# Two key-weight loads on ScalarE's queue, a later gate column, other dummies and a wider last weight load in a two-branch linear attention

## The chip, the cores and the metric

The kernel runs on one core of a Trainium2 chip. The metric is the device time of one launch in microseconds (us); the profile's own clock starts at the first instruction ("span"). Names of the engines in the profile: PE is TensorE's matmul, PEld its weight load, DVE VectorE, ACT ScalarE, POOL GpSimd, SP SyncE. SPq and ACTq are instructions with which SyncE and ScalarE issue transfers (DMAs).

## The reference, cut to what matters

Two branches A and B of linear attention over the same input x (2048 rows, 640 features, 32 heads of 20), mixed by a gate:

```python
def branch(x, wqkv, wo):                       # A_wqkv, A_wo or B_wqkv, B_wo
    q, k, v = split(x @ wqkv)                  # 32 heads of 20
    phi = lambda t: where(t > 0, t + 1, exp(t)) + 1e-6
    pq, pk = phi(q), phi(k)
    kv = einsum("bhsd,bhse->bhde", pk, v)
    z = einsum("bhsd->bhd", pk)
    num = einsum("bhqd,bhde->bhqe", pq, kv)
    den = einsum("bhqd,bhd->bhq", pq, z)[..., None] + 1e-6
    return (num / den) @ wo
g = sigmoid((A_x * gate_w).sum(-1, keepdims=True))
out = g * branch(A_x, A_wqkv, A_wo) + (1 - g) * branch(A_x, B_wqkv, B_wo)
```

All inputs and the output are bf16.

## The kernel before, in words

x is cut into 16 tiles of 128 rows and 5 chunks of 128 features. The kernel needs x both as it is (`XN`) and transposed (`XT`). Tiles 0 and 1 are loaded plainly and transposed on TensorE by a multiplication with a unit matrix (`x_tp`, L478), their copies out of PSUM go to VectorE for tile 0 and to ScalarE for tile 1 (L495). Tiles 2 to 15 are transposed by the DMA (`xt_dma`).

Keys come first. A key step (`k_step`, L534 and L535) multiplies one chunk of one x tile with the 640 key columns of the same chunk of `wqkv` (tile `WKW`), as 512 and 128 columns. For tiles 0 and 1 the steps of branch A run chunk by chunk, both tiles for each chunk, so that each weight chunk is used as soon as it has landed; then branch B does the same. `gate_col` (L515) transposes the gate weights on TensorE, and a copy on VectorE (L518) puts them as a 641st key column beside each chunk's weights; branch B's steps compute the gate's argument with it. From tile 2 on, `k_both` (L612) does both branches at once. `k_post` turns keys into phi(k).

Then, per branch, phi(k) transposed times x gives a matrix of 640 x 641 (`g_unit`, L720 and L721), query tiles are computed between (`q_unit`, L874), and `kv_unit` (L782) multiplies the value weights (`WV`, as the stationary operand, loaded into TensorE in groups of 128 columns) with that matrix: five groups of 120 result columns, and a sixth that is narrower, loaded with 104 columns and 40 result columns. `wp_burst` (L817) folds the result with `wo`, its rows pass through DRAM and come back as `WPA` and `WPB`, and the output matmuls (L1034) follow.

The order is made by a small planner (`Sched`): TensorE runs its instructions in the order of the program text; the other engines choose among what is ready by priority and assumed costs; transfers of the loading phase are issued in program order on their queue. All transfers are issued at L353. SyncE's queue carries nearly all: x tile 0, the five key-weight chunks of A, the five of B, then the transposing loads of x tiles 2 to 15, the rest of x, query, value and output weights. ScalarE's queue carries x tile 1 and the gate weights; behind these on ScalarE stand the activation table's load (L384) and the copies of x tile 1. At the very start TensorE multiplies ones (`warm`, L465): these are dummies, four of 512 columns, one of 256, and one of 128 between the transposes of tile 0 and tile 1. GpSimd clears pads (L399 for `WV`).

```python
    for c in range(NC):
        if c == 0:
            ld_x("SP", c)
        ld_wk("SP", "A", c)
    for c in range(NC):
        ld_wk("SP", "B", c)
```

Of the kernel before, what the change touches and what calls it, by code (L numbers as in the profile page):

```python
# [6 lines left out]
ACT = mybir.ActivationFunctionType  # L7
# [4 lines left out]
D = 640  # L12
# [3 lines left out]
NC = 5  # L16
EPS = 1e-6
XS = ("A", "B")
GR = 120
# [57 lines left out]
class Sched:  # L77
# [7 lines left out]
    def op(self, eng, fn, cost, ins=(), outs=(), after=(), prio=None, name="", dma=None):  # L85
        if eng == "ACT" and dma is None:
            after = list(after) + self.consts
        o = Op(eng, fn, cost, list(ins), list(outs), after, len(self.ops) if prio is None else prio, name, dma)
        self.ops.append(o)
        return o  # L90
# [174 lines left out]
def body(nc, A_x, A_wqkv, A_wo, B_x, B_wqkv, B_wo, gate_w, out, log=None):  # L265
# [7 lines left out]
    bf, f32 = dt.bfloat16, dt.float32  # L273
    sb = nc.alloc_sbuf_tensor
# [3 lines left out]
    WKC = WKW[:, 0 : NC * 2 * KB_W].rearrange("p (c x f) -> p c x f", c=NC, x=2)  # L278
    WK = {X: WKC[:, :, i, :] for i, X in enumerate(XS)}
    WQ = {X: sb("WQ" + X, [128, NC, D], bf) for X in XS}  # L280
    WV = {X: sb("WV" + X, [128, NC, D + 8], bf) for X in XS}
    WO = {X: sb("WO" + X, [128, NU, D], bf) for X in XS}
    PKS = sb("PKS", [128, 2, NT * D], bf)
    PK = {X: PKS[:, i, :] for i, X in enumerate(XS)}
# [23 lines left out]
    PQ["B", 3] = GSf[:, 0:2560].rearrange("p (g s) -> p g s", g=NC)  # L308
    FXT = {"A": WV["A"][:, :, :].rearrange("p c f -> p (c f)")[:, 0:2048].rearrange("p (b s) -> p b s", b=NB), "B": XNf[:, 0:2048].rearrange("p (b s) -> p b s", b=NB)}
    NOA = 15  # L310
# [29 lines left out]
    op = sch.op  # L340

    def psw(b, w):
        return PS[:, b.slot : b.slot + b.n, :].rearrange("p a b -> p (a b)")[:, 0:w]
# [3 lines left out]
    def dma(q, name, dst, src, nbytes, ins=(), outs=(), after=(), issue=450.0, transpose=False, prio=None):  # L347
        timing = (330.0, 1500.0) if not transpose else (140.0, 1500.0) if loading else (1000.0, 1150.0)

        def fn(e):  # L350
            d = dst() if callable(dst) else dst
            with nc.allow_non_contiguous_dma(reason="layout"):
                return e.dma_start(d, src() if callable(src) else src, transpose=transpose)  # L353

        o = op(q, fn, 0.0, ins, outs, after, prio=prio, name=name, dma=(issue, nbytes) + timing)
        if loading:
            o.behind = chain.get(q)
            chain[q] = o
        return o
# [7 lines left out]
    def dve1(n):  # L367
        return 155 + 1.04 * n

    def dve4(n):  # L370
# [22 lines left out]
        outs=[bid],  # L393
        name="idn",
    )
    zgw = op("POOL", lambda e: e.memset(GWZ[:, :], 0.0), 200.0, name="zgw")
    bpad = {X: Buf("pad") for X in XS}
    for X in XS:
        op("POOL", lambda e, X=X: e.memset(WV[X][:, :, 0:4], 0.0), 300.0, outs=[bpad[X]], prio=10**6, name="wvpad")  # L399
    bxo = Buf("xo")  # L400
    op("POOL", lambda e: e.memset(XN[:, :, D : D + 1], 1.0), 200.0, outs=[bxo], name="xones")

    def ld_x(q, t):
        dma(q, "x%d" % t, XN[:, t, 0:D], x[128 * t : 128 * t + 128, :], 163840, outs=[bxn[t]])

    def ld_wk(q, X, c, after=()):
        dma(q, "wk%s%d" % (X, c), WK[X][:, c, 0:D], wqkv[X][128 * c : 128 * c + 128, D : 2 * D], 163840, outs=[bwk[X, c]], after=after)
# [13 lines left out]
    def w3(X, k):  # L421
        return wqkv[X][:, k * D : k * D + D].rearrange("(c p) f -> p c f", p=128)
# [4 lines left out]
    for c in range(NC):  # L427
        if c == 0:
            ld_x("SP", c)
        ld_wk("SP", "A", c)  # L430
    for c in range(NC):
        ld_wk("SP", "B", c)
    for t0, t1 in ((2, 3), (3, 4), (4, 5), (5, 6), (6, 8), (8, 12), (12, 16)):
# [4 lines left out]
    for X in XS:  # L438
        dma("SP", "wv" + X, WV[X][:, :, 4 : D + 4], w3(X, 2), 819200, outs=[bwv[X]])
    for X in XS:  # L440
        for r in range(2):
# [7 lines left out]
                outs=[bwo[X, r]],  # L449
# [11 lines left out]
    def warm(n, w=4):  # L461
        for i in range(n):
            op(
                "PE",
                lambda e: e.matmul(psw(bw, 128 * w), ONE[:, 0:1].to_broadcast([128, 128]), ONE[:, 0:1].to_broadcast([128, 128 * w]), start=True, stop=True),  # L465
                107.0 * w,
                ins=[bone],
                outs=[bw],
                name="warm",
            )  # L470

    def x_tp(t):
        for lo, hi in ((0, 1), (1, 3), (3, 5)):
            bt = Buf("tp", "ps")
            for c in range(lo, hi):
                op(
                    "PE",
                    lambda e, c=c, lo=lo, bt=bt: e.matmul(  # L478
                        PS[:, bt.slot, 128 * (c - lo) : 128 * (c - lo) + 128],
                        XN[:, t, 128 * c : 128 * c + 128],  # L480
                        IDN[:, :],
                        start=True,
                        stop=True,
                    ),
                    100.0,
                    ins=[bxn[t], bid],
                    outs=[bt],
                    name="tp%d" % t,
                )
            half = Buf("xth")  # L490

            def copy(e, lo=lo, hi=hi, bt=bt):
                o = XT[:, lo:hi, 128 * t : 128 * t + 128]
                i = PS[:, bt.slot, 0 : 128 * (hi - lo)].rearrange("p (c s) -> p c s", c=hi - lo)
                return e.activation(o, i, ACT.Copy) if t else e.tensor_copy(o, i)  # L495

            op(
                "ACT" if t else "DVE",
                copy,
                act_cost(128 * (hi - lo)) if t else dve1(128 * (hi - lo)),  # L500
                ins=[bt],
                outs=[half],
                name="tpc%d" % t,
            )
            bxt[t].parts = getattr(bxt[t], "parts", []) + [half] * (hi - lo)
# [3 lines left out]
    def gate_col():  # L509
        bt = Buf("gwp", "ps")  # L510

        def tv():
            return PS[:, bt.slot, 0:NC]

        op("PE", lambda e: e.matmul(tv(), GWZ[:, :], IDN[:, 0:NC], start=True, stop=True), 60.0, ins=[bgw, bid], outs=[bt], name="gwt")  # L515
        op(
            "DVE",
            lambda e: e.tensor_copy(WKC[:, :, :, D : D + 1], tv().unsqueeze(2).unsqueeze(3).to_broadcast([128, NC, 2, 1])),  # L518
            170.0,
            ins=[bt],  # L520
            outs=[bgc],
            name="gwc",
        )
# [143 lines left out]
        clamp(768, 1280, [eb], tb)  # L667
        add(PKt["B"][:, t, 0:512], lambda: bank(2), lambda: ekw(768, 1280), 2, [tb], [pk["B"]])

    warm(4)  # L670
    warm(1, 2)
    pss = [Buf("k", "ps", 2) for _ in range(2)]
    x_tp(0)
    warm(1, 1)
    x_tp(1)
    for c in range(2):
        for t in range(2):
            k_step("A", t, c, pss[t])
    gate_col()
    for c in range(2, NC):  # L680
        for t in range(2):
            k_step("A", t, c, pss[t])
    for t in range(2):
# [7 lines left out]
    for t in range(2, NT):  # L691
# [12 lines left out]
        outs=[bgg2],  # L704
        prio=LOW + 52,
        name="gm",
# [47 lines left out]
    def kv_unit(X):  # L754
        gv = GS[X][:, :, :].rearrange("p c (g m) -> p c g m", g=NC)

        def out(src, u0, n, w, mask, r0, r1):
            b = Buf("kvl")
            bkvl[X].append(b)
            op(  # L760
                "DVE",
                lambda e: e.tensor_tensor(
                    out=KVL[X][r0:r1, u0 : u0 + n, 0 : w * NC].rearrange("p u (m g) -> p u g m", g=NC),
                    in0=src().rearrange("p (u g m) -> p u g m", u=n, g=NC),
                    in1=mask.unsqueeze(1).unsqueeze(1).to_broadcast([r1 - r0, n, NC, w]),
                    op=ALU.mult,
                ),
                dve1(w * NC * n),
                ins=[ps, bcst],
                outs=[b],  # L770
                prio=-1,
                name="kvm",
            )

        for us in ((0, 1, 2, 3), (4, 5)):
            ps = Buf("kv", "ps")

            def fn(e, us=us, ps=ps):
                for i, u in enumerate(us):
                    for c in range(NC):  # L780
                        lo, n, w = (GR * u, 128, 24) if u < 5 else (540, 104, 8)
                        r = e.matmul(  # L782
                            PS[0:n, ps.slot, GR * i : GR * i + NC * w],
                            WV[X][:, c, lo : lo + n],
                            gv[:, c, :, 24 * u : 24 * u + w],
                            start=(c == 0),
                            stop=(c == NC - 1),
                        )
                return r

            o = op("PE", fn, 5 * len(us) * 55.0, ins=[bwv[X], bpad[X]] + [bgs[X, g] for g in range(NC)], outs=[ps], name="kv" + X)
            if X == "A":
                kv_op[X].append(o)
            n = min(us[-1], 4) - us[0] + 1
            out(lambda ps=ps, n=n: PS[:, ps.slot, 0 : GR * n], us[0], n, 24, BDM, 0, 128)
            if 5 in us:
                out(lambda ps=ps: PS[64:104, ps.slot, GR : GR + 40], 5, 1, 8, BDE, 64, 104)
# [427 lines left out]
```

## Time and profile before

| | us |
|---|---|
| device time, median of 3 runs | 187.89 (187.56 to 188.15) |
| span of the profiled execution | 186.1 |
| median less span | 1.8 |
| PE busy in it | 183.1 |
| DVE / ACT / POOL busy | 137.2 / 96.5 / 0.8 |

Of the profiled execution the profile gives the span; the time around it is taken as the difference to the median of the runs. In a line of the timeline the first number is the start in us from the span's start, the second the duration, then the engine, the line of the kernel, the operation, what it writes and reads (`out<-in`), its shape and how many instructions are merged; in brackets stands how long the engine was idle before it, and what ended that. In the chain, each line is a piece of the path that ended last, in order of time. Groups give durations in ns as minimum, median and maximum. Matmul durations overlap, since matmuls are pipelined; the pace is read from the starts.

### The profile page before, as it was taken

How to read it: one execution, taken by the hardware profiler on the slowest of the kernel's cores; microseconds unless marked ns; L12 is line 12 of the kernel's file. 1: busy time of each engine (PE TensorE's matmuls, PEld its weight loads, DVE VectorE, ACT ScalarE, POOL GpSimd, SP SyncE). 2: the span in 40 equal slices, each digit the busy share in tenths (PEclk: the TensorE clock that was granted, in tenths of full speed). 3: DMA queues.
4: the chain of work that ended last, by engine and by line, in shares of the span. 5: the costliest groups of instructions: out<-in, count | busy, mean ns of one | idle time of the engine just before them, and what ended most of it. 6: DMA issues, size and time to landing. Idle time of an engine off the chain costs nothing.

```text
span 186.1 us, 3137 instructions
## 1 busy us (share of the span) xinstructions
PE 183.1 (98%) x1227; PEld 105.2 (57%) x1227; DVE 137.2 (74%) x278; ACT 96.5 (52%) x181; POOL 0.8 (0%) x10
## 2 busy tenths in 40 slices
PE   8999999999999999999999999999999999999995
PEld 4555554555555556555557555555567555555553
DVE  2389888888733555487889899999899998159563
ACT  5266656665554546544675666888623784400001
POOL 1000000000000000000000000000000000000000
DMA  7979999997006011010501402125515247523334
GB/s 203 291 147 166 252 386 365 341 180 153 4 0 39 0 35 35 4 35 16 104 0 39 86 18 46 32 50 162 178 39 118 58 92 170 178 73 113 137 109 140
DMA packets 36501, 21.37 MB, mean 115 GB/s; under 512 B 25694, under 2 KB 36230, under 8 KB 36486
## 3 DMA queue, kind: packets, MB, share of 16 engines
q1 hardware_dynamic: 36188, 20.97, 44.8%
q8 instruction: 9, 0.15, 0.3%
q10 hardware_dynamic: 298, 0.20, 0.3%
q14 instruction: 6, 0.05, 0.1%
HBM read 10.87 MB, written 4.26 MB: 81 GB/s over the span
## 4 chain that ended last, share of the span: by engine, by line
PE 96%; DMA 2%; SPq 1%; DVE 0%; issue 0%; DVEq 0%
PE ps L1034 23%; PE ps L874 23%; PE ps L612 20%; PE ps L720 19%; PE ps L721 5%; DMA WKW<-in_A_wqkv_dram 2%; PE ps L534 2%; PE ps L782 2%; PE ps L817 1%; SPq L353 1%; PE ps L535 0%; DVE TSB L1078 0%; DVEq L237 0%
## 5 line engine op out<-in xcount | busy, mean ns | idle before, releaser
L720 PE MATMUL ps<-XN,PKS 128*128 128x512 bf16 x160 | 46.9, 379 | 0.0
L891 ACT ACTIVATE EK<-ps 128x512 bf16<-128x512 f32 x40 | 23.9, 598 | 30.2 <-PE ps L874 30.2
L612 PE MATMUL ps<-WKW,XT 128*128 128x512 bf16 (+1 forms) x210 | 38.1, 344 | 0.0
L721 PE MATMUL ps<-XN,PKS 128*128 128x129 bf16 x160 | 35.2, 220 | 0.0
L612 PEld LDWEIGHTS ps<-WKW,XT 128*128 128x128 bf16 x210 | 20.3, 97 | 17.5
L720 PEld LDWEIGHTS ps<-XN,PKS 128*128 128x128 bf16 x160 | 18.8, 117 | 15.8
L649 DVE SCALAR_TENSOR_TENSOR PKS<-ps,EK 128x512 bf16<-128x512 f32 (+1 forms) x42 | 24.0, 599 | 1.0
L874 PE MATMUL ps<-XT,WQA 128*128 128x512 bf16 x100 | 24.5, 379 | 0.0
L874 PE MATMUL ps<-XT,WQB 128*128 128x512 bf16 x100 | 23.8, 380 | 0.0
L901 DVE TENSOR_SCALAR EK<-EK 128x512 bf16<-128x512 bf16 x40 | 11.6, 289 | 14.1 <-ACT EK L891 14.0
L721 PEld LDWEIGHTS ps<-XN,PKS 128*128 128x128 bf16 x160 | 18.8, 117 | 3.1
L1034 PE MATMUL ps<-WPA,EX 128*128 128x512 bf16 x120 | 17.0, 299 | 0.0
L1034 PE MATMUL ps<-WPB,PKS 128*128 128x512 bf16 x120 | 16.5, 299 | 0.0
L874 PEld LDWEIGHTS ps<-XT,WQB 128*128 128x128 bf16 x100 | 10.9, 118 | 8.6 <-issue 0.4
L874 PEld LDWEIGHTS ps<-XT,WQA 128*128 128x128 bf16 x100 | 10.6, 117 | 8.1
L1034 PEld LDWEIGHTS ps<-WPB,PKS 128*128 128x128 bf16 x120 | 9.2, 98 | 7.2
L1034 PEld LDWEIGHTS ps<-WPA,EX 128*128 128x128 bf16 x120 | 9.1, 98 | 7.1 <-issue 0.4
L1080 ACT ACTIVATE TSB<-ps 128x512 bf16<-128x512 f32 x1 | 0.6, 597 | 21.9 <-PE ps L1034 21.9
L898 ACT ACTIVATE PKS<-ps 128x512 bf16<-128x512 f32 x20 | 11.9, 595 | 0.0
L639 DVE TENSOR_SCALAR EK<-EK 128x768 bf16<-128x768 bf16 (+1 forms) x28 | 9.0, 321 | 3.9 <-ACT EK L629 3.9
L666 ACT ACTIVATE EK<-ps 128x512 bf16<-128x512 f32 x14 | 8.4, 597 | 6.6 <-PE ps L612 6.6
L625 ACT ACTIVATE EK<-ps 128x512 bf16<-128x512 f32 x14 | 8.4, 597 | 6.4 <-PE ps L612 6.4
(80 smaller groups left out, 199.5 us busy)
## 6 DMA issues: line engine op xcount, KB each, us to landing
out_dram<-TSB SPq DMA_DIRECT2D x15, 160.0 KB, 1.8
XN<-in_A_x_dram SPq DMA_DIRECT2D x1, 2240.0 KB, 9.1
WKW<-in_A_wqkv_dram SPq DMA_DIRECT2D x5, 160.0 KB, 4.1
WKW<-in_B_wqkv_dram SPq DMA_DIRECT2D x5, 160.0 KB, 3.9
WQA<-in_A_wqkv_dram SPq DMA_DIRECT2D x1, 800.0 KB, 10.7
WQB<-in_B_wqkv_dram SPq DMA_DIRECT2D x1, 800.0 KB, 12.0
WVA<-in_A_wqkv_dram SPq DMA_DIRECT2D x1, 800.0 KB, 11.9
WVB<-in_B_wqkv_dram SPq DMA_DIRECT2D x1, 800.0 KB, 13.8
```

What stands on the lines that cost most here:

```text
L612: x = e.matmul(two() if i == 1 else bank(i), XT[:, c, 128 * t : 128 * t + 128], r, start=(c == 0), stop=(c == NC - 1))
L625: op("ACT", lambda e: e.activation(ekw(0, 512), bank(0), ACT.Exp), act_cost(512), ins=[ps[0]], outs=[ek, ea], name="ke")
L639: lambda e: e.tensor_scalar(ekw(lo, hi), ekw(lo, hi), 1.0, EPS, op0=ALU.min, op1=ALU.add),
L649: lambda e: e.scalar_tensor_tensor(dst, src(), 0.0, e1(), op0=ALU.max, op1=ALU.add),
L666: op("ACT", lambda e: e.activation(ekw(768, 1280), bank(2), ACT.Exp), act_cost(512), ins=[ps[2]], outs=[ek, eb], name="ke")
L720: e.matmul(a[:, 0:512], l, XN[:, t, 0:512], start=(t == 0), stop=(t == NT - 1))
L721: return e.matmul(a[:, 512 : D + 1], l, XN[:, t, 512 : D + 1], start=(t == 0), stop=(t == NT - 1))
L874: r = e.matmul(PS[:, ps.slot, :], WQ[X][:, c, g::5], XT[:, c, 512 * b : 512 * b + 512], start=(c == 0), stop=(c == NC - 1),)
L891: lambda e: e.activation(EQ[:, eq.slot, :], PS[:, ps.slot, :], ACT.Exp),
L898: op("ACT", lambda e: e.activation(PQ[X, b][:, g, :], PS[:, ps.slot, :], ACT.Relu), act_cost(512), ins=[ps], outs=[rq], name="qr")
L901: lambda e: e.tensor_scalar(EQ[:, eq.slot, :], EQ[:, eq.slot, :], 1.0, EPS, op0=ALU.min, op1=ALU.add),
L1034: r = e.matmul(a[:, l0 - lo : h0 - lo], PQ[X, b][:, g, 128 * (t % 4) : 128 * (t % 4) + 128], WP[X][:, g, l0:h0], start=(X == first and g = ...
```

## The change

Four edits. (1) Branch A's key-weight chunks 1 and 3 are issued on ScalarE's queue, behind the gate weights; chunks 0, 2 and 4 stay on SyncE's. (2) `gate_col` comes after four chunks of branch A instead of two. (3) The first dummies are five instead of four of 512 columns, followed by the same one of 256; the one of 128 columns between the two tiles' transposes is gone. (4) The last key-value group loads 128 columns instead of 104; `WV` grows by 20 columns, and GpSimd clears a second pad of 24 columns in each branch's `WV`. Its extra result rows are not read.

```diff
-    WV = {X: sb("WV" + X, [128, NC, D + 8], bf) for X in XS}
+    WV = {X: sb("WV" + X, [128, NC, D + 28], bf) for X in XS}
...
-        op("POOL", lambda e, X=X: e.memset(WV[X][:, :, 0:4], 0.0), 300.0, outs=[bpad[X]], prio=10**6, name="wvpad")
+        for lo, hi in ((0, 4), (D + 4, D + 28)):
+            op("POOL", lambda e, X=X, lo=lo, hi=hi: e.memset(WV[X][:, :, lo:hi], 0.0), 300.0, outs=[bpad[X]], prio=10**6, name="wvpad")
...
-        ld_wk("SP", "A", c)
+        ld_wk(("SP", "ACT")[c % 2], "A", c)
...
-    warm(4)
+    warm(5)
     warm(1, 2)
     pss = [Buf("k", "ps", 2) for _ in range(2)]
     x_tp(0)
-    warm(1, 1)
     x_tp(1)
-    for c in range(2):
+    for c in range(4):
         for t in range(2):
             k_step("A", t, c, pss[t])
     gate_col()
-    for c in range(2, NC):
+    for c in range(4, NC):
...
-                        lo, n, w = (GR * u, 128, 24) if u < 5 else (540, 104, 8)
+                        lo, n, w = (GR * u, 128, 24) if u < 5 else (540, 128, 8)
```

## The prediction

> **What bounds the kernel now.** I read the busy table first, then the chain of waits, then the timeline of the first 10 us, then the landings of the key-weight loads.
>
> ```profile
> span 186.1 us, 3137 instructions
> ...
> PE 183.1 (98%) x1227; PEld 105.2 (57%) x1227; DVE 137.2 (74%) x278; ACT 96.5 (52%) x181; POOL 0.8 (0%) x10
> ```
>
> TensorE (PE) is idle for only 3.0 us of 186.1. So a gain must either fill one of these holes or shorten TensorE's own work. The chain says where the holes are:
>
> ```profile
> 0.00 0.40 SPq L353
> ...
> 0.45 0.41 SPq L353
> ...
> 0.91 0.43 SPq L353
> ...
> 1.38 4.14 DMA WKW<-in_A_wqkv_dram
> ...
> 5.57 0.39 PE ps L534
> ```
>
> Up to 5.57 the end of the kernel hangs on SyncE (SP) issuing loads and on the third one, branch A's key-weight chunk 2 (issued at 1.38, landed 4.14 later at 5.52). From 5.57 the chain is TensorE alone until a copy of 0.29 at 184.08. The start is the first place to look. TensorE's part of it in the timeline:
>
> ```profile
> 1.99 0.42 PE L465 MATMUL ps<-ONE 128*128 128x256 bf16 x1
> 2.60 0.69 PE L478 MATMUL ps<-IDN,XN 128*128 128x128 bf16 x5 [0.19 <-DMA XN<-in_A_x_dram]
> 3.08 0.32 PE L465 MATMUL ps<-ONE 128*128 128x128 bf16 x1
> ```
>
> and, in the same timeline, the steps of branch A:
>
> ```profile
> 4.69 0.39 PE L534 MATMUL ps<-WKW,XT 128*128 128x512 bf16 x1 [0.24 <-DMA WKW<-in_A_wqkv_dram]
> ...
> 5.25 0.17 PE L515 MATMUL ps<-IDN,GWZ 128*128 128x5 bf16 x1
> ...
> 5.57 0.39 PE L534 MATMUL ps<-WKW,XT 128*128 128x512 bf16 x1 [0.16 <-DMA WKW<-in_A_wqkv_dram]
> ```
>
> Two stalls: chunk 1 (step starts at 4.69) and chunk 2 (5.57). The gate column's transpose at 5.25 lies inside the second. From 5.57 a key step (512 + 128 columns) comes every 0.27 (five from 5.57 to 6.94), and branch B's first step starts at 7.21.
>
> Landings, each issue time plus its time to landing: chunk 0 0.45+2.9=3.35; chunk 1 0.91+3.7=4.6; chunk 2 5.52; chunk 3 1.86+4.1=5.95; chunk 4 2.33+4.05=6.4; B0 2.81+4.0=6.8; B4 4.70+3.9=8.6; x tile 2 by transpose 5.18+4.1=9.3 (used at 9.94). From chunk 2 on they come about 0.43 apart. The table by stages says whether the DMA engines or the issues set that pace (columns: stretch, length, busy of five engines, clock, DMA share, GB/s):
>
> ```profile
> 2.50:3.00 0.50, 0.40 (x5) 0.43 (x6) 0.10 (x1) 0.23 (x2) 0.00 (x0) 1.00 1.02 368
> 3.00:3.50 0.50, 0.50 (x7) 0.50 (x6) 0.50 (x3) 0.00 (x0) 0.00 (x0) 1.00 1.19 207
> 3.50:4.00 0.50, 0.50 (x7) 0.30 (x5) 0.37 (x2) 0.46 (x2) 0.00 (x0) 1.00 0.66 128
> 4.00:4.50 0.50, 0.45 (x4) 0.12 (x2) 0.00 (x0) 0.41 (x2) 0.00 (x0) 1.00 0.78 264
> ```
>
> From 2.0 to 3.0 about 374 GB/s flow (380, then 368), with ScalarE's queue still delivering x tile 1. Then SP's queue alone feeds the engines, and 3.0 to 4.5 has a hole: mean (207+128+264)/3 = 200. Missing: 174 GB/s x 1.5 us = 0.26 MB, or **0.70 us** at 374. Every later landing carries that delay.
>
> **The change, part by part.** All times are on this execution's span, 186.08; the median of the runs, 187.89, lies 1.81 above it, and I add that at the end.
>
> *Chunks 1 and 3 on ScalarE's queue.* SP issues every 0.47 (0.45, 0.91, 1.38). Two issues fewer bring everything behind them on SP forward: chunk 2 to 0.91, chunk 4 to 1.38, B0 to 1.86, the first transposing load from 5.18 to about 4.24. ScalarE (ACT) issues its loads after the gate weights (0.70+0.52=1.22): chunk 1 at 1.25, chunk 3 at 1.72. Chunk 1 is thus issued 0.34 later than now, chunk 3 0.14 earlier. Behind them on ScalarE stand the table load (1.25, takes 1.28), a 0.20 activation, and the copies of x tile 1 (from 3.54). The table moves to 2.19, the activation ends at 3.68, the first copy starts at 3.70 instead of 3.54; so tile 1's first step goes from 4.02 to about 4.17. Today the 0.24 and 0.16 waits for weights behind it would hide that; if the weights come early, it is what is late next. Branch A then ends no earlier than 4.17 + 9 steps x 0.273 + 0.056 for the gate transpose (the pace of 128 columns, 5.80 to 5.85) = 6.68 against 7.21: **at most 0.53 gained**. B0 must have landed by then (6.8 now, so 0.17 earlier), x tile 2 by 9.4 (9.3 now, and issued 0.9 earlier).
>
> What the landings do is the unknown. *No gain:* the engines are full (share 1.0) and bytes are the same, so 0. *Whole hole filled:* 0.70 earlier, capped to 0.53. *Loss:* chunk 1, first needed, lands behind others (rival 2). The nearest row with loads on both queues is 2.0 to 3.0, without a hole; so I take most of it, 0.52 of 0.70: chunk 2 lands at 5.0, its step starts at 5.05, and six steps and the gate transpose end at 6.75. That is **0.46 gained**; half the hole (0.35) would give 5.23+1.64+0.06=6.93, gain 0.28.
>
> The Trainium skill speaks against this edit: "DMA: Bandwidth & Descriptors", section "Issuing engines are not separate DMA queues", says loads issued by different engines end on the same 16 DMA engines, so that a second issuer saves only issuing time. By that alone this part would be worth about 0 less the gate's 0.06. The hole with engines at shares of 0.66 and 0.78 is why I don't follow it fully.
>
> *Gate column later.* Its 0.056 lay in a stall; now it is on busy TensorE between chunks 3 and 4 (already in the sums). Its copy on VectorE starts 0.21 after it and takes 0.20 (5.25, 5.46, done 5.66); branch B's first step, which needs it, starts 0.056+0.546=0.60 after it. Cover 0.19; without it, 0 to 0.1 lost.
>
> *Dummies.* Five of 512 columns and one of 256 instead of four and one, and the 128-column one at 3.08 goes. They start 0.43 apart, so the 256 one moves from 1.99 to 2.41 and streams 0.21, to 2.62; the transposes begin at about 2.63 instead of 2.60, and the second five at 3.17 instead of 3.19. Zero, unless the pace (128 columns each 0.107 before 3.6, 0.056 later) doubles at another time: each 0.1 us of slow pace costs 0.05 either way. I take 0.
>
> *128 columns in the last key-value group.* 30 matmuls take 1.54 (99.98 to 101.52). 25 of them have 120 columns, at 0.0525 by the pace of 128 columns: 1.31. The five of 40 columns with 104-column loads take 0.23, 0.046 each.
>
> ```profile
> L782 PEld LDWEIGHTS ps<-GSA,WVA x30: 97/98/128, 99.8 to 101.4; 128*128 128x128 bf16 x25, 128*104 128x104 bf16 x5
> L782 PE MATMUL ps<-GSA,WVA x30: 183/216/217, 100.0 to 101.5; 128*128 128x120 bf16 x25, 128*104 128x40 bf16 x5
> ```
>
> The narrower load is the longer one, 128 ns against 98. This combination isn't in the trace: at worst 0.0525 each as beside 120 columns (0.03 lost per unit), at best the stream of 40 columns, 0.0175 (0.14 gained). Loads 30 ns shorter bring 0.046 near that end; I take 0.10, twice (branch A at 100, branch B at 141.6), **0.20**; both ends: -0.06 to 0.28. The Trainium skill, "TensorE: Matmul & The Clock Gate", section "Weight-path perf modes — Fast Weight Load (FWL) and DoubleRow", says the fast load is on at 128 weights, which fits the two rows; its floor of 25 ns between small matmuls (section "Wait — 56ns, not 53.3ns?") would make it 0.21 for both units as an estimate.
>
> *Pads.* Two more memsets on GpSimd of 0.11 to 0.14 each, 0.2 busy in all before 1.5; first needed at 99.8. Zero.
>
> *What is late next downstream.* The tightest load: WPB is issued at 156.66 and lands 4.4 later at 161.06; its first weight load is at 161.6. If the VectorE and SP work before it didn't move along, only some 0.5 of the gain would pass; most of it is released by TensorE and moves. I charge 0.
>
> **Sum:** 0.46+0.20=0.66; 186.08-0.66+1.81 = **187.2**.
>
> **Rivals.** *1, bandwidth decides:* the hole comes from what the packets wait for, whichever queue they are on. Chunk 2 still lands at 5.52; the start loses 0.06, the key-value units give 0.20: 187.75. For it: the DMA share is about 1.0 from 2.0 to 3.0 and after 4.5, and the hole's 1.19 in its first half us means packets that take long. Against: the hole begins when only one queue is left. *2, chunk 1 falls behind (slower):* its later issue and a shared turn on the engines let chunks 2, 4 and perhaps B0 pass. In fifth place (5.52) branch A ends at 5.57+8x0.273+0.06=7.81, 0.60 late, net +0.40: 188.3. In sixth (5.95): 8.24, net +0.83: **188.7**. It decides, beyond 0.3% (0.56 us, about what a measurement of this kernel can tell from no change), once chunk 1 lands after 5.7. For it: it is issued 0.34 later, behind x tile 1 and the gate weights. Against: x tile 1, issued on ScalarE at 0.12, landed only 0.4 after x tile 0. *3, the 128-column load brings nothing:* forecast less 0.20: 187.4.
>
> **Chances.** Forecast 0.55 (its own range 187.0 to 187.5, part of it within 0.3%), rival 1 0.25, rival 2 0.13, rival 3 0.07. Faster by over 0.3% (under 187.33): 0.48, 0.45 of it the forecast's and 0.03 of rival 3. Slower by over 0.3%: 0.10, rival 2 from the sixth place on. The rest, 0.42, within. The range starts at the full caps (0.53+0.28, 187.08, less 0.1 for the pace) and ends at rival 2's milder form: 187.0 to 188.3.
>
> **What would show it.** Right: chunk 2's step before 5.1, branch B's first step at 6.7 to 6.8, no DMA wait behind 4.5, no stretch of 0.5 us under 250 GB/s between 3 and 4.5; last key-value matmuls under 0.03 apart; first ScalarE copy at 3.7. Wrong: chunk 2 at 5.5 again (rival 1), a wait for chunk 1 longer than 0.5 (rival 2), a wait for the gate copy before branch B, a wait for WPB at 161.

## The result and the profile after

The changed kernel is slower: 190.58 us (189.19 to 191.14, six runs) against 187.61 (187.21 to 188.15, six runs of the kernel before on the same chip), a ratio of 1.0148 [1.0126, 1.0170]; the medians differ by 2.97 us. Ratios, here and below, compare mean times and leave out launches more than 1.5% above the same kernel's fastest, which are two of e0's and one each of e5's, e7's and e9's. The forecast was 187.2, and the time lies above the range. The profiled execution took 190.29 with a span of 188.9, 2.8 longer than the span before. First the page's total and busy times and the start of the chain of waits of the changed kernel:

```profile
span 188.9 us, 3117 instructions
...
PE 183.7 (97%) x1204; PEld 106.0 (56%) x1227; DVE 137.2 (73%) x278; ACT 96.4 (51%) x181; POOL 1.1 (1%) x12
```

```profile
1.25 5.02 DMA WKW<-in_A_wqkv_dram
6.40 0.59 PE ps L535
```

The chain no longer begins with SyncE's issues. It hangs on chunk 1, which ScalarE issues at 1.25 and which lands 5.02 later at 6.27; before, it landed at 4.65. TensorE's timeline in the changed kernel, over the first steps (`L535` is the 512-column matmul of a key step; the first line is chunk 0's second step, the others lie behind the wait for chunk 1):

```profile
4.25 0.63 PE L535 MATMUL ps<-WKW,XT 128*128 128x512 bf16 x1
...
6.40 0.59 PE L535 MATMUL ps<-WKW,XT 128*128 128x512 bf16 x1 [1.41 <-DMA WKW<-in_A_wqkv_dram]
...
6.89 0.63 PE L535 MATMUL ps<-WKW,XT 128*128 128x512 bf16 x1
...
7.43 0.63 PE L535 MATMUL ps<-WKW,XT 128*128 128x512 bf16 x1
...
9.63 0.41 PE L535 MATMUL ps<-WKW,XT 128*128 128x512 bf16 x1
...
9.93 0.38 PE L535 MATMUL ps<-WKW,XT 128*128 128x512 bf16 x1
...
10.20 0.38 PE L535 MATMUL ps<-WKW,XT 128*128 128x512 bf16 x1
```

The last line is branch B's first step. In the kernel before it is this one:

```profile
7.21 0.38 PE L534 MATMUL ps<-WKW,XT 128*128 128x512 bf16 x1
```

Two things are to be seen. TensorE idles 1.41 us for chunk 1. And the steps behind it begin 0.53 apart (6.89 to 7.43) until about 9.6, and 0.27 apart (9.93 to 10.20) only from there; before, they were 0.27 apart from the third step on. Branch B's first step starts at 10.20 instead of 7.21, 2.99 later. The key-value units give 0.1 each back, and 2.99 - 0.2 is the 2.8 of the spans. With chunk 1 at 6.40 and the pace of 0.27, branch B would have begun at 6.40 + 8 x 0.27 + 0.06 = 8.6: so 1.4 of the 2.99 is **late weights** and 1.6 is **slow pace**.

The stages of the changed kernel in which the kernel before had its hole (columns as before; the last two are the DMA share and GB/s), then the last of these stages in the kernel before:

```profile
3.00:3.50 0.50, 0.50 (x7) 0.50 (x6) 0.50 (x2) 0.49 (x2) 0.00 (x0) 1.00 1.06 202
3.50:4.00 0.50, 0.50 (x5) 0.37 (x4) 0.47 (x2) 0.50 (x3) 0.00 (x0) 1.00 0.93 115
4.00:4.50 0.50, 0.50 (x3) 0.26 (x2) 0.00 (x0) 0.41 (x2) 0.00 (x0) 1.00 0.50 138
4.50:5.00 0.50, 0.49 (x2) 0.00 (x0) 0.00 (x0) 0.00 (x0) 0.00 (x0) 1.00 0.74 220
```

```profile
4.50:5.00 0.50, 0.31 (x3) 0.19 (x4) 0.00 (x0) 0.00 (x0) 0.00 (x0) 1.00 0.93 338
```

The hole was to be filled by the second queue. In this launch it is deeper and longer: from 3.0 to 5.0 the DMA engines move 338 KB ((202+115+138+220)/2) instead of 468 KB ((207+128+264+338)/2). All later landings slip: chunk 2 5.90 (5.53 before), chunk 4 6.76 (6.38), chunk 3 7.19 (5.95), branch B's five from 7.39 (6.80) on. Of the 16 landings that the trace has for each chunk, chunk 2's have their median at 3.69 and the last at 5.90: a few parts are late, and a chunk counts from its last part.

The last edit did what it was to do. The groups of the value-weight matmuls, branch A:

```profile
L782 PEld LDWEIGHTS ps<-GSA,WVA x30: 95/98/98, 102.8 to 104.4; 128*128 128x128 bf16 x30
L782 PE MATMUL ps<-GSA,WVA x30: 179/216/216, 103.0 to 104.4; 128*128 128x120 bf16 x25, 128*128 128x40 bf16 x5
```

No load of 128 ns is left, the five matmuls of 40 columns start 0.025 to 0.028 apart (0.029 to 0.049 before), and the unit's piece of the chain takes 1.43 instead of 1.52.

### The profile page after: what moved, and what is told of

Same layout as the page of the kernel before. It is cut to its first block, busy times and chain, and to the rows that moved or that the text cites. A ratio compares the mean times of both kernels' runs of the same rounds, so it can differ in the third digit from the quotient of the medians.

```text
span 188.9 us, 3117 instructions
## 1 busy us (share of the span) xinstructions
PE 183.7 (97%) x1204; PEld 106.0 (56%) x1227; DVE 137.2 (73%) x278; ACT 96.4 (51%) x181; POOL 1.1 (1%) x12
## 4 chain that ended last, share of the span: by engine, by line
PE 95%; DMA 3%; issue 1%; POOL 0%; DVE 0%; POOLq 0%; DVEq 0%
PE ps L1034 23%; PE ps L874 23%; PE ps L613 20%; PE ps L720 18%; PE ps L721 5%; PE ps L535 3%; DMA WKW<-in_A_wqkv_dram 3%; PE ps L782 2%; PE ps L817 1%; PE ps L536 1%; POOL IDN L388 0%; DVE TSB L1078 0%; POOL WVA L400 0%; POOL XN L402 0%; POOL const-float32-0.0 L1210 0%
## 5 line engine op out<-in xcount | busy, mean ns | idle before, releaser
L720 PE MATMUL ps<-XN,PKS 128*128 128x512 bf16 x154 | 45.8, 379 | 0.1
L1034 PE MATMUL ps<-WPA,EX 128*128 128x128 bf16 (+1 forms) x117 | 16.6, 297 | 0.3 <-issue 0.2
L1034 PE MATMUL ps<-WPB,PKS 128*128 128x512 bf16 (+1 forms) x117 | 16.3, 297 | 0.2
```

What stands on the lines that cost most here:

```text
L720: e.matmul(a[:, 0:512], l, XN[:, t, 0:512], start=(t == 0), stop=(t == NT - 1))
L1034: r = e.matmul(a[:, l0 - lo : h0 - lo], PQ[X, b][:, g, 128 * (t % 4) : 128 * (t % 4) + 128], WP[X][:, g, l0:h0], start=(X == first and g = ...
```

## The experiments

Theory 1: the whole loss comes from the queue edit, by two terms, the late chunks and a slow pace that the idle time at 4.7 to 6.4 keeps. Its rivals: the new dummies or the later gate column hold the pace down; the pace is the launch's luck. Later runs ask why the chunks land late: because two queues share the engines, because ScalarE issues late, or because of the gate weights. Ratios are to the kernel before, measured beside each. Single launches of 684 us (e1), 243 us (e14) and 193.5 us (the kernel before, beside e8, e9 and e11) are left aside.

**e1: the queue edit alone**, on the kernel before.

```diff
-        ld_wk("SP", "A", c)
+        ld_wk(("SP", "ACT")[c % 2], "A", c)
```

> The kernel before with the first edit alone: chunks 1 and 3 of branch A on ScalarE's queue. Theory 1 (the queue does it all, in two terms): the chunks of both queues share the engines and land together late (chunk 1 at about 6.3 instead of 4.6), worth +1.4 us, and TensorE's idle hole before it keeps its pace slow, worth up to another +1.6. Then 190.3 to 190.9 us, near the changed kernel plus the 0.2 that its key-value units gain. Rival (the dummies or the later gate column do part of it): below 189.5 us.

Measured 188.68, ratio 1.0068 [1.0038, 1.0098]. The queue edit alone costs, but 1 us, not 3. In its profile chunk 1's step waits 0.85 and starts at 6.01, the pace is already 0.27 there, and branch B starts at 8.22. One of seven launches took 190.48. So the late chunks cost something in each of the seven (the lowest is 188.17, the median of the kernel before 187.65), the slow pace shows in one: that half of the expectation fell.

**e2: the change without the queue edit.**

```diff
-        ld_wk(("SP", "ACT")[c % 2], "A", c)
+        ld_wk("SP", "A", c)
```

> The changed kernel with all key-weight chunks back on SyncE's queue; the later gate column, the longer dummies and the 128-column load stay. Theory 1: 187.3 to 187.6 us, 0.0 to 0.3 below the kernel before (0.2 gained in the key-value units, 0.06 lost on the gate column). Rival (dummies or gate column cost something): above 188.2 us.

Measured 187.45, ratio 0.9990 [0.9969, 1.0011]. Gate column, dummies and wide load together cost nothing that can be told from zero.

**e3: the change with dummies in the idle time**, three of 512 columns between the steps of chunk 0 and those of chunk 1.

```diff
             k_step("A", t, c, pss[t])
+        if c == 0:
+            warm(3)
```

> The changed kernel with three more dummies of 512 columns on TensorE between the steps of chunk 0 and chunk 1, where it stood idle from 4.8 to 6.4. The loads are untouched. Theory 1 (idling keeps the pace slow): the landings stay late, but the pace doubles by 7.1 in every run: 188.9 to 189.4 us, 1.2 to 1.6 below the changed kernel, and the runs lie within 0.8 us. Rival (the pace has nothing to do with the idle stretch, or the loss is all in the landings): 190.3 to 190.8 us, no change.

Measured 188.72 (188.10 to 189.12), ratio 1.0057 [1.0038, 1.0076]. No launch is near 190.6. What is left, 1.1, is the late chunks less the key-value gain. Since e1, measured beside it, has only one of seven launches near 190.6, these six alone don't settle the pace; e7 and e14 do.

**e4: the wide load alone**, with its second pad, on the kernel before.

```diff
-    WV = {X: sb("WV" + X, [128, NC, D + 8], bf) for X in XS}
+    WV = {X: sb("WV" + X, [128, NC, D + 28], bf) for X in XS}
...
-                        lo, n, w = (GR * u, 128, 24) if u < 5 else (540, 104, 8)
+                        lo, n, w = (GR * u, 128, 24) if u < 5 else (540, 128, 8)
```

> The kernel before with the fourth edit alone, the 128-column load of the last key-value group and its pads. Theory: each key-value unit takes 1.43 instead of 1.52 to 1.54 us, both lie on TensorE's path: 0.2 us less, 187.4 us. Rival (what the units give is lost in a wait later): no difference within 0.1 us.

Measured 187.31, ratio 0.9982 [0.9969, 0.9994], which is 0.34 less, with 0.11 to 0.58 in the interval. The 0.20 of the prediction lies in it. This is the only kernel of the study whose interval lies wholly below the kernel before.

**e0 and e13: the changed kernel twice more**, later and on two chips.

> The changed kernel once more, beside the others on one chip. With the first edit alone the time was 188.7 us, where 190.3 to 190.9 was expected, and TensorE's pace doubled at 4.9 there and at 9.6 in the changed kernel. Theory 2 (the pace doubles at a moment that the program does not fix; the idle hole before chunk 1 only decides whether a late one costs): runs fall into two groups, about 188.3 to 189.2 us and about 190.2 to 191.2 us, and the share of each differs from the first measurement. Rival (edits 2 to 4 together with the queue cost 1.8 us): all runs at 190.2 to 191.2 us.

> The changed kernel a third time, beside e14. Theory 2: two groups of launches again, about 187.9 to 189.2 and 190.2 to 191.2 us; how many fall in each is not predicted.

Measured 188.89, ratio 1.0052 [1.0036, 1.0068] (1.0078 with its two launches near 191 counted), and 188.91, ratio 1.0077 [1.0046, 1.0109]: by the medians the same kernel costs 1.1 to 1.3 over the kernel before there, not 3. The launches fall in two groups: up to 189.2 and from 189.8 on. Of the first six, five are in the upper one; of e0's nine, two (190.84, 191.03); of e13's eight, three. The timeline of e0's profiled launch (188.65), from the second step of chunk 0:

```profile
4.23 0.63 PE L535 MATMUL ps<-WKW,XT 128*128 128x512 bf16 x1
...
6.35 0.38 PE L535 MATMUL ps<-WKW,XT 128*128 128x512 bf16 x1 [1.38 <-DMA WKW<-in_A_wqkv_dram]
...
6.62 0.38 PE L535 MATMUL ps<-WKW,XT 128*128 128x512 bf16 x1
```

Chunk 1 is as late as in the first profile, but the next step follows after 0.27: the pace doubled during the idle time. Branch B begins at 8.54.

**e7: a hole without the queue edit.** On the kernel before, chunk 1's first step also waits for chunk 4; all loads stay as they were.

```diff
-            ins=xin + [bwk[X, c]] + ([bgc] if X == "B" else []),
+            ins=xin + [bwk[X, c]] + ([bwk["A", NC - 1]] if (X, t, c) == ("A", 0, 1) else []) + ([bgc] if X == "B" else []),
```

> The kernel before, in which the first step of chunk 1 also waits for chunk 4 (landed at about 6.4), so that TensorE stands idle from 4.3 or 4.8 to 6.4; loads, queues and dummies are as before. By the landings alone branch B's first step moves from 7.21 to 6.43+8x0.273+0.06=8.67, +1.46: 189.1 us in every run. Theory 2 (the hole can also hold the pace down): two groups, about 188.6 to 189.4 us and about 190.2 to 191.2 us. Rival (the slow pace of the changed kernel comes from ScalarE's queue or the dummies): one group at 189.1 us.

Measured 190.51 (188.87 to 191.78), ratio 1.0117 [1.0081, 1.0152], again two groups: two launches at 188.9, four from 190.3 on. Its profiled launch took 190.81; TensorE's timeline, then the stages of that launch (after the stretch and its length: PE, PEld, DVE, ACT, POOL, granted clock, DMA share, GB/s):

```profile
4.09 0.38 PE L534 MATMUL ps<-WKW,XT 128*128 128x512 bf16 x1
...
6.69 0.38 PE L534 MATMUL ps<-WKW,XT 128*128 128x512 bf16 x1 [2.17 <-DMA WKW<-in_A_wqkv_dram]
...
6.96 0.58 PE L534 MATMUL ps<-WKW,XT 128*128 128x512 bf16 x1
...
10.55 0.38 PE L534 MATMUL ps<-WKW,XT 128*128 128x512 bf16 x1
```

```profile
7.00:8.00 1.00, 1.00 (x8) 0.45 (x6) 0.20 (x1) 0.00 (x0) 0.00 (x0) 0.51 1.35 339
8.00:9.00 1.00, 1.00 (x6) 0.45 (x5) 0.00 (x0) 0.00 (x0) 0.00 (x0) 0.50 1.00 176
9.00:10.00 1.00, 1.00 (x5) 0.48 (x4) 0.00 (x0) 0.00 (x0) 0.00 (x0) 0.50 1.06 214
```

The pace was fast at 4.09 and for the first step behind the hole; then the granted clock falls to 0.50 and stays there until about 10.4, some 3.4 us. So idling by itself, with no load moved, can cost TensorE its pace. In the profile of the changed kernel the clock's column shows 1.00 throughout, though the steps are 0.53 apart: there the steps are slow on both sides of the idle time, so that no fast pace is seen to be lost, and only the starts show it. Both forms stand in the upper group: of the changed kernel's ten launches above 189.7, six have a mean granted clock of 0.991, which is 3.4 us at half pace in 190, and four have 1.000, as the profiled one.

The Trainium skill, "TensorE: Matmul & The Clock Gate", section "Part 1: The HAM clock gate (the "warmup" mystery)", says that the clock is judged in windows of about 3.4 us that run freely against the launch, that an idle window halves it, and that the moment therefore varies. The length of the slow stretch here (3.4) and the two groups agree with it; what these runs add is that idle times of 1.4 us (to hold the slow pace) and 2.2 us (to fall back to it), shorter than that window, are enough in some launches.

**e14: e7 with the hole filled**, by four dummies of 512 columns with a PSUM bank of their own.

```diff
+        if c == 0:
+            bw = Buf("warm", "ps")
+            warm(4)
```

> As e7 (the first step of chunk 1 waits for chunk 4 too), with four dummies of 512 columns on TensorE in the hole; loads as in the kernel before. Theory 2 (idling holds the pace down): no launch above 189.8 us, all within about 188.5 to 189.6, where e7 had four of six at 190.3 to 191.8. Rival (the two groups have another cause): as e7, half or more of the launches above 190.2 us.

```profile
4.70 1.38 PE L465 MATMUL ps<-ONE 128*128 128x512 bf16 x4
6.28 0.38 PE L534 MATMUL ps<-WKW,XT 128*128 128x512 bf16 x1 [0.20 <-DMA WKW<-in_A_wqkv_dram]
...
6.54 0.38 PE L534 MATMUL ps<-WKW,XT 128*128 128x512 bf16 x1
```

Measured 189.03 (188.76 to 189.15), ratio 1.0068 [1.0047, 1.0089]. This timeline shows the dummies, the short wait left, and full pace after it. With the hole filled the upper group is gone, as in e3: of the eleven launches of both none is above 189.2. Of the changed kernel's 23 launches ten are above 189.7, of e7's six four; e13, measured beside e14, has three of its eight there. Of the other kernels whose profile shows a wait of 0.85 us or more before chunk 1, e1 has one of seven, e5 three of six, e9 four of six, e12 one of twelve and e11 none of twelve above 189.7; e2, e4, e6 and e8, with shorter waits, have none of 47 above 188.3. So such a wait makes the slow pace possible, not certain.

**e5: branch B's chunks 1 and 3 on ScalarE instead of A's**, behind the gate weights, on the kernel before.

```diff
-        ld_wk("SP", "B", c)
+        ld_wk(("SP", "ACT")[c % 2], "B", c)
```

> The kernel before with chunks 1 and 3 of branch B, not A, on ScalarE's queue behind the gate weights. Branch A's issues stay where they are on SyncE's queue; B's chunks are needed only from 7.2 on. Theory 1 (packets of two queues take turns on the same engines): A's chunks 1 to 4 land later than before although they are issued as early, chunk 1 after 5.2, chunk 4 after 6.8; 188.2 to 190.0 us. Rival (A's chunks were late in the changed kernel because ScalarE issues later): chunk 1 at about 4.6 and chunk 4 at about 6.4 as before; 187.4 to 187.9 us.

TensorE's timeline in e5, chunk 1 and chunk 2:

```profile
5.77 0.39 PE L534 MATMUL ps<-WKW,XT 128*128 128x512 bf16 x1 [0.90 <-DMA WKW<-in_A_wqkv_dram]
...
7.13 0.39 PE L534 MATMUL ps<-WKW,XT 128*128 128x512 bf16 x1 [0.64 <-DMA WKW<-in_A_wqkv_dram]
```

Measured 189.65 (188.61 to 191.46), ratio 1.0100 [1.0062, 1.0138]. A's five loads are all issued by SyncE as before, yet chunk 1 lands at 5.72 (4.65 before) and chunk 2 at 7.08 (5.53). So here loads on the other queue that nobody needs yet delayed those needed now.

**e6: the change with ScalarE's two chunks ahead of the gate weights.**

```diff
     ld_x("ACT", 1)
-    dma("ACT", "gw", GWZ[0:NC, :], gate_w.rearrange("(c p) -> c p", p=128), 1280, outs=[bgw], after=[zgw])
...
         ld_wk(("SP", "ACT")[c % 2], "A", c)
+    dma("ACT", "gw", GWZ[0:NC, :], gate_w.rearrange("(c p) -> c p", p=128), 1280, outs=[bgw], after=[zgw])
```

> The changed kernel with ScalarE's chunks 1 and 3 issued ahead of the gate weights, so that chunk 1 is issued at about 0.55 instead of 1.25, earlier than in the kernel before (0.91). Theory 1 (turns on the engines): all of chunks 1 to 4 still land late, chunk 4 or 3 after 6.8, chunk 1 perhaps earlier than 6.0; 188.0 to 190.5 us. Rival (late issue): chunk 1 by 4.2, chunks 2 to 4 as in the kernel before or earlier; 187.2 to 187.7 us.

ScalarE's issues in e6 (the changed kernel issues the gate weights at 0.70 and the chunks from 1.25), then the stages of e6:

```profile
0.54 0.93 ACTq L353 DMA_DIRECT2D WKW<-in_A_wqkv_dram  x2
1.51 0.57 ACTq L353 DMA_DIRECT2D GWZ<-in_gate_w_dram  x1
```

```profile
3.00:3.50 0.50, 0.50 (x9) 0.42 (x7) 0.47 (x2) 0.49 (x2) 0.00 (x0) 1.00 1.09 284
3.50:4.00 0.50, 0.45 (x5) 0.26 (x4) 0.50 (x2) 0.50 (x4) 0.00 (x0) 1.00 0.97 282
4.00:4.50 0.50, 0.36 (x4) 0.02 (x1) 0.00 (x1) 0.33 (x2) 0.00 (x0) 1.00 0.95 316
```

Measured 187.37, ratio 0.9989 [0.9975, 1.0003]. The loss is gone, the hole too (294 GB/s on average from 3.0 to 4.5 against 200). Chunk 1's step starts at 4.58. Yet branch B still starts at 7.21, as before: the chunk in fourth place, 3, lands at 5.97 (5.95 before), and the last, 4, only 0.25 earlier. What is left of e6's gain is the key-value units'. So even a filled hole is not worth the 0.46.

**e8: is it the gate weights?** The change with all chunks on SyncE, and the gate weights issued behind the table load (`tab`), at 2.13 instead of 0.70.

```diff
-    dma("ACT", "gw", GWZ[0:NC, :], gate_w.rearrange("(c p) -> c p", p=128), 1280, outs=[bgw], after=[zgw])
+    dma("ACT", "gw", GWZ[0:NC, :], gate_w.rearrange("(c p) -> c p", p=128), 1280, outs=[bgw], after=[zgw, tab])
...
-        ld_wk(("SP", "ACT")[c % 2], "A", c)
+        ld_wk("SP", "A", c)
```

> All key-weight chunks on SyncE's queue and edits 2 to 4 (as in e2), but ScalarE issues the gate weights only after its table load, at about 2.1 instead of 0.7. In every trace so far with the gate weights issued at 0.7 the DMA rate falls to 100 to 230 GB/s from 3.0 to 4.5; with them issued at 1.5 (e6) it stayed at 280 to 316. Theory 3 (the small gate load on ScalarE's queue makes that hole and holds up what is behind it): the hole is gone or later, chunk 2 lands before 5.2; 187.0 to 187.3 us, 0.2 to 0.4 below e2's 187.45. Rival (the hole belongs to the chunks): hole at 3.0 to 4.5 as before, 187.3 to 187.6 us.

Measured 187.55, ratio 0.9988 [0.9975, 1.0001]. The hole is still there (144 and 152 GB/s in the stages from 3.0 to 4.0), so the gate weights don't make it.

**e9: late, but with no gate weights ahead.** As e6, but ScalarE's first chunk waits for the last pad, and the activation table's load stands behind the gate weights.

```diff
+        ld_wk(("SP", "ACT")[c % 2], "A", c, after=[pad] if c == 1 else ())
+    dma("ACT", "gw", GWZ[0:NC, :], gate_w.rearrange("(c p) -> c p", p=128), 1280, outs=[bgw], after=[zgw])
+    tab.behind = chain["ACT"]
```

> As e6 (ScalarE issues chunks 1 and 3 and only then the gate weights), but the issue of chunk 1 waits for GpSimd's last pad, so that it comes at about 1.45, later than in the changed kernel (1.25). Theory 3 (the gate load ahead is the trouble): no deep hole, chunk 1 lands by about 5.0; 187.2 to 187.9 us. Rival (the late issue lets SyncE's chunks pass): chunk 1 after 5.7, 188.3 to 190.8 us like the changed kernel.

The issue and chunk 1's step in e9 (its `L536` is the 512-column matmul):

```profile
1.44 0.83 ACTq L353 DMA_DIRECT2D WKW<-in_A_wqkv_dram  x2
```

```profile
6.57 0.39 PE L536 MATMUL ps<-WKW,XT 128*128 128x512 bf16 x1 [1.38 <-DMA WKW<-in_A_wqkv_dram]
```

Measured 190.04 (188.88 to 192.01), ratio 1.0100 [1.0069, 1.0131]. The table load thus moved to 2.91, and tile 1's step of chunk 0 begins at 4.62 instead of 4.25; chunk 1 comes two us later than that, so this hides. Issued at 1.44, chunk 1 lands at 6.53 without the gate weights ahead of it.

**e12: in between.** As e9, but the first chunk waits for the unit matrix (`idn`), which puts its issue at 1.02.

```diff
-        ld_wk(("SP", "ACT")[c % 2], "A", c)
+        ld_wk(("SP", "ACT")[c % 2], "A", c, after=[idn] if c == 1 else ())
+    dma("ACT", "gw", GWZ[0:NC, :], gate_w.rearrange("(c p) -> c p", p=128), 1280, outs=[bgw], after=[zgw])
+    tab.behind = chain["ACT"]
```

> As e6 and e9 (ScalarE issues chunks 1 and 3, then the gate weights), but chunk 1 waits for the unit matrix on GpSimd and is issued at about 1.0: 0.54 in e6 was good, 1.44 in e9 bad. If the moment of issue alone decides, and gradually, chunk 1 lands between e6's 4.4 and e9's 6.5 and the time lies between, 187.6 to 189.0 us. If it decides by a threshold (ScalarE's queue must get the chunk while x tile 1 still keeps it busy, to about 2.5 with a delay of 1.1 to 1.4 from issue to first packet), 1.0 is still in time: 187.2 to 187.8 us, chunk 1 by 4.8.

Measured 188.02, ratio 1.0028 [1.0004, 1.0053]; chunk 1's step at 5.85, chunk 3's waits another 0.28 at 7.39. The time lies between e6 and the change. The profiled launch (188.62) is one of the slower of the twelve.

**e11: e5 with B's chunks ahead of the gate weights**, issued from 0.54.

```diff
-    dma("ACT", "gw", GWZ[0:NC, :], gate_w.rearrange("(c p) -> c p", p=128), 1280, outs=[bgw], after=[zgw])
...
-        ld_wk("SP", "B", c)
+        ld_wk(("SP", "ACT")[c % 2], "B", c)
+    dma("ACT", "gw", GWZ[0:NC, :], gate_w.rearrange("(c p) -> c p", p=128), 1280, outs=[bgw], after=[zgw])
```

> As e5 (branch B's chunks 1 and 3 on ScalarE's queue), but ahead of the gate weights instead of behind them. The chunks of both branches share the engines even earlier than in e5. Theory 3 (the gate load ahead is the trouble): A's chunk 4 lands clearly before e5's 7.7, and the time falls from 189.65 to below 188.6 us. Rival (sharing alone did it): A's chunks land as late as in e5 or later, 189.0 to 191 us.

Measured 187.95, ratio 1.0014 [0.9995, 1.0034]: most of e5's loss is gone. Chunk 1 is still late (its step at 5.56, after a wait of 1.09), but the later chunks of A are there when their steps come. The time is what was expected of the gate weights as the cause; since e9 excludes them, what e11 shares with e6 is the early issue.

One table holds the study together: where branch B's first step starts in eleven of the sixteen profiled launches, and that launch's span.

| kernel | ScalarE's first chunk issued | KB moved 3.0 to 5.0 | chunk 1's step | branch B's first step | span |
|---|---|---|---|---|---|
| before | none | 468 | 4.69 | 7.21 | 186.1 |
| e2 | none | 455 | 4.45 | 7.20 | 185.9 |
| e6 | 0.54 | 608 | 4.58 | 7.21 | 185.9 |
| e12 | 1.02 | 440 | 5.85 | 8.52 | 187.2 |
| e3 | 1.24 | 482 | 5.79 | 8.00 | 186.7 |
| e1 | 1.24 | 413 | 6.01 | 8.22 | 187.2 |
| e0 | 1.25 | 332 | 6.35 | 8.54 | 187.2 |
| e13 | 1.24 | 341 | 6.77 | 8.97 | 187.7 |
| after | 1.25 | 338 | 6.40 | 10.20 | 188.9 |
| e9 | 1.44 | 372 | 6.57 | 8.78 | 187.5 |
| e7 | none | 480 | 6.69 | 10.55 | 189.4 |

Span less branch B's start is 178.7 in every row that has the wide load and 178.9 to 179.0 in the three that have not. So nothing downstream gives back or adds anything: a microsecond lost at the start is one at the end. The KB of 3.0 to 5.0 don't follow the loss: with ScalarE's chunks issued at 1.24 to 1.25 they are low in four launches (332 to 413) but not in e3 (482), while chunk 1 is late in all five, its step at 5.79 to 6.77.

## Why the prediction was wrong

*Chunks 1 and 3 on ScalarE's queue: this step failed.* "I take most of it, 0.52 of 0.70: chunk 2 lands at 5.0" and "0.46 gained" had the wrong sign: chunk 2 landed at 5.90, chunk 1 at 6.27, and branch B could start no earlier than about 8.6, a loss of 1.4 (1.3 and 1.8 in the launches of e0 and e13, which kept the fast pace). The reasoning was that the hole begins where only one queue is left, so a second one would fill it. The row it rested on (2.0 to 3.0, two queues at 374 GB/s) was of loads issued at 0.0 to 0.5. In the runs the loss goes with the time of the issue: 0.54 fills the hole and costs nothing (e6), 1.02 costs 0.3% (e12), 1.25 and 1.44 cost 0.5 to 1.5% (e0, e13, after, e9). And where the hole was filled, the needed chunks came hardly earlier (e6), so that the estimate fails from that side too.

*The page against it.* The section of the Trainium skill that the prediction weighed ("DMA: Bandwidth & Descriptors", "Issuing engines are not separate DMA queues": a second issuer saves only issuing time) would have given this edit 0. So it is with e6. Issued as in the change, the edit alone costs 1.0 (e1), which neither the page nor the prediction had.

*Rival 2* named the mechanism of the first term: chunk 1 issued 0.34 later falls behind the others. Its sign, a wait for chunk 1 longer than 0.5, is there (1.41). It landed behind chunk 2 only (5.90, then 6.27), but all of them were late, so that it came 0.32 later than the prediction's worst place (5.95). "In sixth (5.95): 8.24 ... 188.7" agrees with what launches at full pace took: medians of 188.75 (the seven lower of e0) and 188.72 (e3). Part of that is luck: the 8.24 is 0.3 early (8.54 in e0), and the 1.81 added to the span is 0.4 too much for e0's profiled launch (188.65 less 187.2). The chance of 0.13 was too small: "x tile 1, issued on ScalarE at 0.12, landed only 0.4 after x tile 0" spoke of early loads again.

*The pace: mis-sized.* "Zero, unless the pace ... doubles at another time: each 0.1 us of slow pace costs 0.05 either way. I take 0." The rule is right and the size was not thought through: once a wait leaves TensorE idle, the slow stretch can be not 0.1 but some 3.2 us (6.40 to 9.6), which cost 1.6. Rival 2 gave the wait but not this consequence of it; with it, rival 2 reads 188.7 + 1.6 = 190.3, inside the upper group (189.8 to 191.1). That idling is the cause is shown by e7 against e14, and e3 agrees; why five of the first six launches but only five of the 17 later ones had it is not settled.

*Gate column, dummies, pads: right.* No wait for the gate's copy appears; the transposes began at 2.70 (2.63 foreseen), ScalarE's first copy at 3.55 (3.70 foreseen); e2 shows the lot at 0.9990, with the wide load in it. *128 columns in the last group: right*, 0.1 per unit in every row of the table that has it. *Downstream: right*, nothing was late next.

*Open:* why the rate falls at 3.0 to 4.5 at all, and why chunks that ScalarE issues after 1 us land so late. In the traces single packets of 1,280 bytes then take up to 1.04 us (before) and 1.78 us (after), and in both each chunk waits for a few of its 16 parts. What such a packet waits for isn't in the trace. The gate weights are excluded (e8, e9). One row separates the kernels: from 2.6 to 3.0 ScalarE's queue moved 64 packets in e6 and 81 in e11, but 0 to 12 in the eight others with chunks on it. So in e6 and e11 the chunk followed x tile 1 on that queue without a break, and in the others SyncE's queue had the engines nearly to itself there. Whether this break or the moment of the issue makes the loss, no run here tells apart.

The change to keep is e4, the wide load alone. e6 and e2 contain it and are not told apart from the kernel before.

## What to carry to other kernels

A load on a second queue is not a free lane: ask how early it is issued (0.54 us was free here, 1.25 was not), and what lands later because of it, also on the queue that isn't touched. Price every wait added to TensorE's first microseconds twice, once for the wait and once for the pace that idling costs behind it; dummies put into such a wait took the second part away here (e3, e14). In this kernel, which TensorE bounds, a delay at the start was paid in full at the end.

## What the runs showed of the hardware

- The pace of TensorE doubles at another moment in each launch: at about 3.6 (before), 4.9 (e1), 4.7 (e12) and 9.6 (after), though dummies ran from 0.3 on in all of them.
- Once doubled it can be lost: 2.17 us of idling in e7 were followed, after one fast step, by 3.4 us at a granted clock of 0.50. The clock's column showed this fall, but not the slow stretch at the start of the changed kernel; the starts of the matmuls show both.
- Two of branch A's chunks on a second queue, issued from 1.24 or 1.25 us, landed late in each of five profiled launches: chunk 1 at 5.74 to 6.64, against 4.32 to 4.97 in the six profiled kernels without a second queue for chunks. From 3.0 to 5.0 the DMA engines then moved 332 to 413 KB in four of the five and 482 in e3, against 434 to 482 in those six; issued at 0.54, 608 KB (e6).
- A weight load of 104 columns takes 128 ns, one of 128 columns 98 ns; the wider one made the unit 0.1 us shorter for five loads.
